# Window attention feeding a mixture of attention experts: odd value slots copied on the engines instead of by transfers, first queries and keys in longer rows, and a new work list

## The chip, the core and the metric

The kernel runs on one core of a Trainium2 chip. The core has five engines, each with an instruction stream of its own that it works through in order: TensorE (PE in the profile, its weight loads PEld), VectorE (DVE), ScalarE (ACT), GpSimd (POOL) and SyncE (SP), which here issues transfers. Matrix results land in PSUM, everything else lies in SBUF. The metric is the device time of one execution in microseconds; three executions of the kernel before gave 263.87, 266.73 and 267.94 us.

## The reference, cut to what matters

Eight batches of 576 tokens, eight heads of 64 numbers. The first half is attention in a window of 32 tokens to either side; its output, heads side by side, is the `x` (576 x 512) of the second half, a layer of four causal attention experts of which each token uses two.

```python
mask = np.abs(pos[:, None] - pos[None, :]) <= 32
attn = softmax(where(mask, scale * q @ k.T, -1e9))
x = heads_side_by_side(attn @ v)                 # (8, 576, 512)
logits = x @ w_gate                              # two best of 4 experts, softmax over the two
for e in range(4):
    q, k, v = x @ wq[e], x @ wk[e], x @ wv[e]
    ye = softmax(causal(scale * q @ k.T)) @ v @ wo[e]
    out += gate[e] * ye
```

All inputs and the output are float32 in the chip's main memory (HBM).

## The kernel before, in words

**One list sets all order.** `ORDER` is a string of some 900 steps. A step such as `sc010@26` names a function, its batch and indices, and after `@` the PSUM banks that it uses and, for a copy, the engine (`v` VectorE, `a` ScalarE, `g` GpSimd). The loop at L602 calls the functions in that order, so every engine's stream is the list filtered to that engine. Waits between engines follow from the data. PSUM is four tiles of two banks, numbered 0, 2, 4 and 6.

**One batch goes through these steps.** `lq`, `lk` load four heads (a group) of q or k into `qn`, `kn`, one row of 18 tokens (4608 bytes) per partition. `tq`, `tk` turn them with VectorE transposes into `Tqn`, `Tkn`, of which there is one buffer for each group. `sc` makes half of a group's scores (32-row matmuls, four in parallel), into two PSUM tiles; `ex` takes the exponential on ScalarE into `A`, once for each tile; `mk` multiplies with the window's mask, mostly on GpSimd. `lv` loads v. `av` multiplies `A` with `V` for 128 tokens, `un` divides by the row sum on VectorE (into `XN`), `xt` transposes on TensorE, `xf` evicts to `XTF`, `xb` rounds to bf16 `XTB`. Then the experts: `ga`, `gt`, `ge`, `gm`, `gu` are the gate; `pp` and `pe` project to queries and keys and evict them; `pv` and `ve` make the values; `ps`, `xe`, `se` are scores, exponential and the causal cut (GpSimd); `po`, `oe`, `pt`, `ot` are the weighted values, their normalising (VectorE), a transpose and its eviction; `py`, `ye`, `st` are the output projection, its eviction and the store. Batches overlap: while the experts of one batch run, the window attention of the next ones is under way.

**The value slots.** `V` has eight slots of 128 partitions. Even slot 2m holds tokens 128m to 128m+127 (`lv` m from 0 to 3); the lower half of slot 7 holds the last 64 tokens (`lv` 4). `av` needs windows that start in the middle of such a block, so odd slot 2m+1 holds in its upper 64 partitions those of slot 2m, and in its lower 64 those of slot 2m+2. `vc(b, x)` at L275 fills the odd slots of one half with two transfers from SBUF to SBUF. Each copies both the 64 numbers of a head and the two columns of ones behind them.

**Transfers are paced.** `load` at L174 issues on SyncE's queue and adds a dependence on the last TensorE instruction that stands before it in the list. A load so starts no sooner than TensorE has come to its place, and every load behind it on SyncE's queue waits too. The stores `st` are on the same queue.

**The start.** Group 0 of batch 0 is loaded with eight transfers each for q (ScalarE's queue) and k (SyncE's), in pieces of three tokens (768 bytes) per partition: `lqa`, `lqb`, `lka`, `lkb`, turned by `tqa` and so on (L297). Group 1 follows with the ordinary `lk01`, `tk01`, `lq01`, `tq01`. `s_mask` builds the mask on GpSimd; `s_pads` and `s_ones` are memsets on VectorE; `s_warm` loads ScalarE's table for the exponential.

Of the kernel before, what the change touches and what calls it, by code (L numbers as in the profile page):

```python
# [24 lines left out]
    s_mask lqa s_pads tqa lka tka lkb tkb s_ones lqb tqb lk01 tk01 lq01 sc000@02 tq01 lq10 lk10 sc001@46  # L25
    s_warm ex0010@4 ex0000@0 ex0011@6 ex0001@2 lq11 lv03 lv02 sc010@26 sc011@04 lk11 lv01 ex0101@6 ex0111@4
    ex0110@0 ex0100@2 vc01 tq10 tk10 mk0000@g mk0111@g mk0010@g mk0101@g lv04 mk0110@v tq11 lv00 wl1 vc00
    wl0 mk0011@g sc100@04 sc101@26 ex1011@6 ex1010@2 s_ident tk11 mk0100@v ex1000@0 ex1001@4 mk1001 mk1011
    av02@2 un02@2 lv10 av03@4 un03@4 mk0001@v av04@0 xt01@4 av00@2 xf01@4a un04@0 cw1@v un00@2 lv13 lv12
    lq20 av01@0 mk1000 mk1010 xt02@4 un01@0 xt00@0 xf02@4v xb01@v xb02@v cw0@v xf00@0a sc111@42 lv11 xb00@v  # L30
    sc110@60 vc11 lv14 tq20 ex1111@2 ex1110@4 ex1100@6 ex1101@0 lk20 pp010@2 pp011@6 pp000@0 pp001@4
    pe000@0v pe010@2a pe011@6a vc10 ga0@2 gt0@2 gm0@2 mk1111 mk1110 mk1101 mk1100 pe001@4a lk21 ps002@4
    ps011@0 ps013@6 xe013@6 xe011@0 ge0@2 av14@3 xe002@4 av13@6 av12@0 un14@3 gu0@2 un13@6 xt12@2 wl2
    ps010@4 xf12@2a un12@0 xe010@4 ps000@6 ps001@2 xt11@0 tk20 xe001@2 xe000@6 lq21 av11@4 sc201@26 xf11@0a
    ex2011@6 un11@4 tk21 wl3 ps003@4 xe003@4 se003 mk2011 se001 lk30 lv22 ex2010@2 cw2@a av10@0 sc200@46
    ps012@2 ex2001@6 ex2000@4 un10@0 xt10@0 xe012@2 xf10@0a lv23 lv20 lv21 tq21 xb12@v pv00@6 ve00@6a se000
    sc210@24 xb10@v xb11@g ex2101@4 mk2001 mk2000 mk2101 pv01@0 pv11@1 tk30 ve11@1v ex2100@2 pp100@6
    pe100@6a lq30 ga1@2 sc211@64 se011 lq31 cw3@a ve01@0a gt1@2 mk2010 gm1@2 ge1@2 gu1@2 pv10@0 vc20 po000@2
    ex2111@4 ex2110@6 ve10@0a vc21 pp111@6 tq30 pp101@0 oe000@2 pe101@0v se010 se013 mk2111 lv24 pe111@6a
    sc301@64 pp110@2 mk2110 lk31 lv30 ex3011@4 ex3010@6 ps101@4 ps102@0 tq31 pe110@2a mk2100 av20@6 un20@6  # L40
    av21@2 un21@2 xe102@0 xe101@4 av22@0 ps110@6 xe110@6 un22@0 lv32 lv34 sc300@24 lk40 tk31 av23@0 un23@0
    ex3001@4 ex3000@2 ps103@4 ps100@6 av24@2 xe103@4 xe100@6 pt000@3 ot000@3v lv33 un24@2 po010@4 ps112@6
    ps113@0 lq41 lq40 xt20@2 xe113@0 xe112@6 xf20@2a mk3001 xt21@0 oe010@4 pt010@4 ot010@4v xt22@5 xf22@5v
    xb22@v xf21@0a sc310@26 ex3100@2 ex3101@6 lk41 lv41 vc31 xb21@v sc311@40 ex3110@4 tk40 tq40 se101 py00@2
    se103 se100 py01@6 ye00@2a se113 ex3111@0 ye01@6a mk3011 mk3000 xb20@g pp210@4 pp201@2 pe210@4a pe201@2a
    pp200@0 tq41 pp211@4 pe211@4v po100@2 st01 lv31 pe200@0a ps202@0 xe202@0 sc400@46 oe100@2 ex4000@4 lk50
    lv42 ga2@2 ps211@4 ps111@0 ex4001@6 tk41 ps203@6 mk3101 xe203@6 mk3010 se111 mk3100 mk3111 mk3110 av34@3
    xe211@4 xe111@0 se110 se203 mk4001 vc30 gt2@2 un34@3 gm2@2 av33@6 av32@4 py02@3 un33@6 un32@4 lq51 st00
    xt32@0 pt100@1 po110@6 pv20@4 ge2@2 xf32@0a ye02@3v oe110@6 gu2@2 ot100@1a lq60 pt110@3 ot110@3v ve20@4a
    xt31@6 ps200@2 xf31@6v sc401@40 xe200@2 lq50 pv21@6 ex4011@0 xb31@v tk50 av30@2 lk60 ps201@0 ex4010@4  # L50
    ve21@6a xe201@0 un30@2 ps212@4 av31@6 py11@0 xe212@4 un31@6 lk51 st02 lv44 sc411@42 ye11@0a lv43 se201
    tq50 py10@6 ex4110@4 ex4111@2 ye10@6v xt30@0 xf30@0a sc410@24 ex4101@4 ex4100@2 sc500@60 lv51 vc41
    ps210@4 ex5000@6 ex5001@0 xe210@4 xb30@v tq51 se200 xb32@g pp301@2 pe301@2a pp300@6 pp311@0 mk4000
    mk4111 lv40 pe311@0a pe300@6a pp310@2 pe310@2a tk51 sc501@04 lv53 ga3@2 ps213@6 gt3@2 ex5010@0 ex5011@4
    ps301@0 xe213@6 ps302@4 se211 py12@3 xe301@0 ge3@2 xe302@4 st11 vc40 lv54 lk61 gm3@2 mk4010 mk4011
    mk4110 mk5001 av43@6 un43@6 gu3@2 se210 av42@0 ye12@3a un42@0 se213 mk4101 po200@4 po210@6 oe200@4
    pv30@2 oe210@6 st10 pt200@0 ot200@0v xt41@4 ve30@2a ps303@0 ps310@6 xf41@4a mk4100 mk5010 mk5000 xe310@6
    av40@2 av41@4 lv52 lq70 lv50 av44@6 lv64 lq61 xe303@0 vc50 un40@2 ps313@2 ps312@0 xe313@2 xe312@0 vc51
    un41@4 un44@6 pt210@7 st12 xt40@4 xb41@g ot210@7v xt42@6 xf40@4a xb40@g mk5011 xf42@6v xb42@v sc511@02
    ex5111@2 ex5110@0 sc510@46 mk5110 ex5101@6 ex5100@4 mk5100 se311 pp401@2 ps311@6 pe401@2a xe311@6  # L60
    ps300@0 xe300@0 ga4@4 se300 mk5101 py21@2 tq60 ye21@2a pv40@6 ve40@6a pp400@2 pp411@0 tk61 gt4@4 ge4@4
    gm4@4 tk60 gu4@4 tq61 lv61 pe400@2a ps403@2 xe403@2 ps401@6 mk5111 ps400@4 av54@2 pe411@0a se303 se310
    se301 xe400@4 xe401@6 av51@0 un54@2 pv31@3 av52@4 un51@0 un52@4 av53@6 ve31@3a av50@0 pv41@2 ve41@2a
    un53@6 se403 se313 st21 py22@3 ye22@3a sc600@64 un50@0 lv62 lv60 ex6000@6 ex6001@4 sc610@20 ex6100@2
    ex6101@0 ps402@6 xt50@4 lv63 lq71 lv74 st22 xe402@6 xf50@4a mk6001 po300@2 se400 xb50@g po310@0 xt51@6
    pp410@4 oe300@2 xf51@6a xt52@2 oe310@0 pt310@3 xf52@2v pe410@4a sc601@60 xb52@v ot310@3a ex6011@0
    sc611@24 ex6110@2 ex6010@6 ex6111@4 mk6100 xb51@g lk70 vc60 vc61 pp501@0 py20@2 ye20@2a pe501@0a mk6011
    pp500@6 pe500@6a mk6110 mk6111 ga5@4 ps413@0 xe413@0 ps412@2 tq70 tq71 xe412@2 ps410@6 lv70 st20 pt300@5
    gt5@4 ot300@5v gm5@4 lv73 pp511@0 se401 mk6010 se413 se411 mk6101 ge5@4 xe410@6 pe511@0a po400@2 oe400@2
    py31@6 mk6000 gu5@4 pp510@0 ye31@6a tk70 ps501@2 pe510@0a xe501@2 ps502@6 ps411@4 av63@0 un63@0 xe502@6  # L70
    xe411@4 av62@2 av61@6 py32@0 ye32@0a st32 un62@2 av60@4 un61@6 pv51@0 ps503@6 ps500@2 un60@4 lk71 lv72
    vc71 st31 xe503@6 av64@1 xe500@2 ve51@0v sc701@46 ex7011@6 ex7010@4 un64@1 xt62@0 xf62@0v xt60@2 xf60@2a
    xt61@6 ps511@4 ps510@0 se500 se410 po410@2 oe410@2 xb62@g xb60@g xf61@6a xb61@v tk71 xe511@4 xe510@0
    mk7010 se501 se503 pv50@6 ve50@6a pt410@0 sc700@24 ex7000@2 ex7001@4 pt400@1 po500@6 mk7011 mk7001
    mk7000 oe500@6 ot400@1v py30@2 ye30@2a ot410@0a lv71 st30 vc70 pp610@4 pp611@6 pe610@4v pe611@6a
    sc711@02 ex7111@2 ex7110@0 sc710@64 mk7111 mk7110 ex7101@4 ps610@2 pp600@0 pp601@4 ex7100@6 mk7100
    mk7101 xe610@2 pe600@0a pe601@4v ps512@2 ps611@6 xe512@2 xe611@6 av73@0 pv61@4 av72@2 un73@0 py42@5
    ps612@0 ps602@6 ve61@4a un72@2 xe612@0 av74@4 un74@4 ye42@5v xe602@6 av70@2 av71@0 un70@2 un71@0 ps513@6
    ps600@4 xe513@6 ga6@2 xe600@4 se511 se601 ps613@0 ps601@6 xe613@0 ps603@4 xe603@4 xt72@3 xe601@6 py41@0
    ye41@0a st41 xf72@3v py40@4 gt6@2 ye40@4v xt71@6 xt70@0 pt500@3 gm6@2 ge6@2 xf71@6a xf70@0v se513 se613  # L80
    se510 xb70@v xb72@g se603 se610 gu6@2 xb71@g se600 se611 pv60@4 po510@0 oe510@0 pp700@6 pe700@6v ve60@4a
    pp701@4 pp711@0 ot500@3a pt510@2 ot510@2v pp710@6 pe710@6v pe701@4a pe711@0a ps702@2 st42 st40 ps703@0
    py51@4 ye51@4v xe702@2 xe703@0 py50@6 po600@0 ps713@4 oe600@0 ye50@6a ps700@2 xe713@4 xe700@2 py52@6
    po610@4 ye52@6v pt600@7 ps701@2 oe610@4 ot600@7v xe701@2 ps712@0 xe712@0 se713 se700 se711 ga7@6 ps711@2
    ps710@4 xe710@4 pt610@7 gt7@6 pv70@0 ot610@7a ge7@6 gm7@6 gu7@6 xe711@2 ve70@0v st50 st51 py61@4 ye61@4a
    st52 se701 se710 se703 pv71@2 py60@6 ye60@6a ve71@2v po711@0 po712@2 po702@4 oe711@0 oe712@2 oe702@4
    py62@0 pt712@1 po701@2 st61 oe701@2 pt702@4 ye62@0a st60 ot702@4v pt701@0 pt711@5 ot711@5v ot701@0v
    ot712@1a py71@2 ye71@2a st62 py70@0 st71 ye70@0a st70 py72@2 ye72@2v st72
"""


@with_exitstack
def kernel(
    ctx: ExitStack,
    tc: tile.TileContext,
    q: bass.AP,
# [9 lines left out]
    nc = tc.nc  # L106
# [196 lines left out]
    def lka():  # L303
        first_load("kn", k, nc.sync, 0, 4)
# [334 lines left out]
```

## Time and profile before

| | |
|---|---|
| median of three executions | 266.73 us |
| the profiled execution, its own time | 266.66 us |
| its span from first to last instruction | 264.9 us |
| TensorE, VectorE, ScalarE, GpSimd busy | 221.9, 182.2, 148.0, 124.4 us |
| first matmul | 9.30 us |
| mean granted TensorE clock | 0.945 |
| transfers from SBUF to SBUF (`V<-V`) | 32 issues: 24 of 264 KB, 8 of 132 KB |

The page gives busy time for each engine, the span in 40 slices (6.6 us each), the groups of instructions, and the chain of work that ended last. The trace answers for any stretch in microseconds from the span's start. The profiled execution lies at the median; 1.8 us of its time lie outside the span.

### The profile page before, as it was taken

To read this page: it belongs to the slowest core of one execution; us is meant where nothing else is said; L and a number is where in the kernel's file an instruction comes from. 1 tells how busy PE (TensorE), PEld (TensorE's weight loads), DVE (VectorE), ACT (ScalarE), POOL (GpSimd) and SP (SyncE) were. 2 spreads that over 40 slices of the span, in tenths; PEclk is the share of its full clock that TensorE was granted. 3 is DMA by queue.
4 is the path that set the end of the run, shared out by engine and by line. 5 is a ranking of instruction groups with operands and counts; after the bars stand their busy time and mean duration, and the time that the engine had idled before them with its cause. 6 is when DMAs were issued, how large, how long until landed. Compare 5 with 4: busy or idle time off the path is not lost.

```text
span 264.9 us, 12355 instructions
## 1 busy us (share of the span) xinstructions
PE 221.9 (84%) x5536; PEld 177.6 (67%) x5536; DVE 182.2 (69%) x385; ACT 148.0 (56%) x223; POOL 124.4 (47%) x137
## 2 busy tenths in 40 slices
PE   0556599799898899997999895999799999998872
PEld 0545478578777668875779864887587877776540
DVE  6988756599888489888627758638673916666650
ACT  0151315569655576475583675277677786556712
POOL 5029543408760677408835394057805864331200
PEclk9985958999999999999799998899999999999987
DMA  6797897998997588988469786075915570314234
GB/s 151 224 299 195 203 206 192 229 249 241 214 244 192 147 289 202 246 305 239 113 178 252 200 206 182 2 186 166 272 30 152 153 191 5 126 55 181 72 111 178
DMA packets 60405, 48.22 MB, mean 182 GB/s; under 512 B 46016, under 2 KB 48576, under 8 KB 60352
## 3 DMA queue, kind: packets, MB, share of 16 engines
q1 hardware_dynamic: 59456, 46.84, 65.0%
q8 instruction: 43, 0.70, 1.1%
q10 hardware_dynamic: 896, 0.59, 0.9%
q14 instruction: 10, 0.08, 0.1%
HBM read 30.42 MB, written 9.44 MB: 150 GB/s over the span
## 4 chain that ended last, share of the span: by engine, by line
PE 65%; DVE 12%; DMA 9%; issue 5%; ACT 3%; SPq 3%; POOL 1%; ACTq 0%; DVEq 0%
PE PS L169 57%; PE PS L172 8%; DMA V<-in_v_dram 5%; SPq L176 2%; DMA kn<-in_k_dram 2%; DMA V<-V 2%; DVE Tkn L286 1%; ACT ATE L529 1%; DVE XTB L157 1%; DVE OE L557 1%; DVE Tqn L286 1%; DVE VE L157 1%; DVE XN L389 1%; ACT OTT L153 1%; DVE OTT L157 1%
## 5 line engine op out<-in xcount | busy, mean ns | idle before, releaser
L363 POOL TENSOR_TENSOR A<-A,MASKP 128x576 f32<-128x576 f32 x61 | 86.6, 1442 | 55.7 <-ACT A L359 55.7
L169 PE MATMUL PS<-Tqn,Tkn 32*64 32x128 f32 (+2 forms) x2560 | 48.2, 284 | 17.5 <-DVE PS L203 9.3
L529 ACT ACTIVATE ATE<-PS 128x1024 bf16<-128x1024 f32 (+1 forms) x64 | 51.1, 842 | 18.5 <-PE PS L169 15.7
L169 PEld LDWEIGHTS PS<-Tqn,Tkn 32*64 32x64 f32 x2560 | 42.6, 146 | 23.3 <-DVE PS L203 9.3
L359 ACT ACTIVATE A<-PS 128x576 f32<-128x576 f32 x64 | 37.7, 652 | 30.2 <-PE PS L169 29.4
L536 POOL TENSOR_SCALAR_AFFINE_SELECT ATE<-ATE 128x512 bf16<-128x512 bf16 (+1 forms) x48 | 24.6, 533 | 54.2 <-ACT ATE L529 54.2
L169 PE MATMUL PS<-V,A 128*64 128x65 f32 (+1 forms) x1280 | 43.1, 231 | 6.7 <-issue 4.1
L169 PEld LDWEIGHTS PS<-V,A 128*64 128x64 f32 (+1 forms) x1280 | 39.4, 139 | 10.8 <-issue 7.1
L286 DVE STREAM_TRANSPOSE Tqn<-qn 128x576 f32<-128x576 f32 x30 | 34.6, 1241 | 4.8 <-DMA qn<-in_q_dram 2.8
L286 DVE STREAM_TRANSPOSE Tkn<-kn 128x576 f32<-128x576 f32 x30 | 34.9, 1241 | 2.0 <-DMA kn<-in_k_dram 2.0
L153 ACT COPY XTF<-PS 128x1024 f32<-128x1024 f32 (+1 forms) x18 | 15.0, 855 | 18.1 <-PE PS L172 17.9
L169 PE MATMUL PS<-WO,OTT 128*128 128x512 bf16 (+1 forms) x96 | 20.8, 365 | 4.2 <-ACT ATE L529 1.5
L389 DVE TENSOR_TENSOR XN<-PS,RC 128x512 f32<-128x512 f32 x32 | 22.1, 691 | 1.1
L172 PE MATMUL PS<-ident,XN 128*128 128x128 f32 x144 | 20.6, 284 | 1.8 <-DVE OTT L157 0.6
L153 ACT COPY Y<-PS 128x1024 f32<-128x1024 f32 (+1 forms) x17 | 14.7, 863 | 11.3 <-PE PS L169 5.7
L153 ACT CAST QKE<-PS 128x576 bf16<-128x576 f32 x25 | 15.8, 651 | 7.3 <-PE PS L169 7.3
L169 PE MATMUL PS<-WV,XTB 128*128 128x256 bf16 (+1 forms) x192 | 18.8, 259 | 0.6 <-issue 0.4
L169 PE MATMUL PS<-QKE 64*128 64x64 bf16 (+4 forms) x192 | 17.0, 280 | 2.7 <-DVE G L477 2.7
L172 PEld LDWEIGHTS PS<-ident,XN 128*128 128x128 f32 x144 | 16.1, 144 | 4.6 <-DVE XN L389 1.4
L169 PE MATMUL PS<-XTB,WQ 128*128 128x288 bf16 x128 | 18.5, 286 | 0.8 <-DVE XTB L157 0.7
L169 PE MATMUL PS<-XTB,WK 128*128 128x288 bf16 x128 | 18.2, 288 | 0.0
L169 PE MATMUL PS<-VE,ATE 128*128 128x65 bf16 x480 | 17.3, 193 | 1.1 <-issue 0.5
(68 smaller groups left out, 232.1 us busy)
## 6 DMA issues: line engine op xcount, KB each, us to landing
kn<-in_k_dram SPq DMA_DIRECT2D x15, 576.0 KB, 5.1
qn<-in_q_dram SPq DMA_DIRECT2D x15, 576.0 KB, 5.2
V<-in_v_dram SPq DMA_DIRECT2D x32, 256.0 KB, 4.5
out_dram<-Y SPq DMA_DIRECT2D x16, 512.0 KB, 3.7
V<-V SPq DMA_DIRECT2D x24, 264.0 KB, 4.2
V<-V SPq DMA_DIRECT2D x8, 132.0 KB, 4.5
V<-in_v_dram SPq DMA_DIRECT2D x8, 128.0 KB, 5.2
out_dram<-Y SPq DMA_DIRECT2D x16, 64.0 KB, 2.9
```

The costliest lines, as they stand in the source:

```text
L153: nc.scalar.copy(o, i)
L157: nc.vector.tensor_copy(o, i)
L169: PACE[0] = nc.tensor.matmul(*args, **kw)
L172: PACE[0] = nc.tensor.transpose(*args)
L176: ins = nc.sync.dma_start(o, i)
L286: nc.vector.transpose(T[:, dh, :].rearrange("q (p o) -> q o p", o=18), n_[:, :, 32 * dh:32 * dh + 32])
L359: nc.scalar.activation(a_part(b, g, half, p), two(b0)[:, :, 0:HS], EXP, scale=scale_att)
L363: (nc.gpsimd if eng == "g" else nc.vector).tensor_tensor(out=ap, in0=ap, in1=MASK[:, None, HS * half:HS * half + HS].to_broadcast([128, 2, ...
L389: nc.vector.tensor_tensor(out=XN[T // 2][:, T % 2, :].rearrange("p (g h d) -> p g h d", g=2, h=4), in0=u[:, :, :, 0:64], in1=rc[:, :, :, N ...
L529: nc.scalar.activation(A[:, at:at + 2 * step].rearrange("p (e x) -> p e x", e=2)[:, :, 0:w], two(b0)[:, :, 0:w], EXP, scale=scale_moe)
L536: nc.gpsimd.affine_select(ap, ap, pattern=[[0, n], [1, w]], compare_op=IS_GE, fill=0.0, base=64 * j if c == 3 else 0, channel_multiplier=-1)
L557: nc.vector.tensor_tensor(out=OE[j][:, t0:t1, :, :].rearrange("p t e d -> p e t d"), in0=p_[:, :, :, 0:64], in1=rg[:, :, :, None].to_broad ...
```

## The change

Three edits of functions, and a new list.

```diff
-    def vc(b, x):
-        pairs = VSB[b % 2][:, :, :, :].rearrange("p (m o) h d -> p m o (h d)", o=2)
-        load(pairs[64:128, 2 * x:2 * x + 2, 1, :], pairs[64:128, 2 * x:2 * x + 2, 0, :])
-        n = 2 - x
-        load(pairs[0:64, 2 * x:2 * x + n, 1, :], pairs[0:64, 2 * x + 1:2 * x + 1 + n, 0, :])
+    def vc(b, x, eng):
+        pairs = VSB[b % 2][:, :, :, :].rearrange("p (m o) h d -> p m o h d", o=2)
+        n = 2 - x
+        copy(eng, pairs[64:128, 2 * x:2 * x + 2, 1, :, 0:64], pairs[64:128, 2 * x:2 * x + 2, 0, :, 0:64])
+        copy(eng, pairs[0:64, 2 * x:2 * x + n, 1, :, 0:64], pairs[0:64, 2 * x + 1:2 * x + 1 + n, 0, :, 0:64])
...
+    FIRST = {"qn": ((0, 9), (9, 18)), "kn": ((0, 10), (10, 18))}
+    def first_load(nm, src, q_, g, x):
+        o0, o1 = FIRST[nm][x]
+        t = NAT[nm][g][:, :, :].rearrange("p o d -> p (o d)")
+        q_.dma_start(t[:, 64 * o0:64 * o1], src[0, 4 * g:4 * g + 4, 32 * o0:32 * o1].rearrange(
+            "h (p o) d -> h p (o d)", p=32))
+    def first_turn(nm, g, x):
+        o0, o1 = FIRST[nm][x]
+        for dh in range(2):
+            nc.vector.transpose(QKT[nm][g][:, dh, 32 * o0:32 * o1].rearrange("q (p o) -> q o p", p=32),
+                                NAT[nm][g][:, o0:o1, 32 * dh:32 * dh + 32])
+    def fk(g, x):
+        first_load("kn", k, nc.sync, g, x)
+    def fq(g, x):
+        first_load("qn", q, nc.scalar, g, x)
+    def gk(g, x):
+        first_turn("kn", g, x)
+    def gq(g, x):
+        first_turn("qn", g, x)
...
             for i in range(2):
-                nc.sync.dma_start(out[b, 512:576, 256 * i:256 * i + 256], ysb(b, w)[64 * i:64 * i + 64, 0, 0:256])
+                (nc.scalar if b == B - 1 and i else nc.sync).dma_start(
+                    out[b, 512:576, 256 * i:256 * i + 256], ysb(b, w)[64 * i:64 * i + 64, 0, 0:256])
```

`vc` is now two engine copies of 64 partitions (1024 numbers each, or 512 for the second one of x = 1), of the 64 numbers alone; the ones stay from a memset. Of its 16 steps the list gives 11 to GpSimd and 5 to ScalarE. Both groups of batch 0 are loaded with `fq` on ScalarE's queue and `fk` on SyncE's, one transfer for a half: 288 tokens of q (9 in a row), 320 and 256 of k (10 and 8 in a row). The second half of the very last store goes through ScalarE's queue.

The list has the same TensorE steps in another order, with other banks. Its first steps were

```
s_mask lqa s_pads tqa lka tka lkb tkb s_ones lqb tqb lk01 tk01 lq01 sc000@02 tq01 lq10 lk10 sc001@46
s_warm ex0010@4 ex0000@0 ex0011@6 ex0001@2 lq11 lv03 lv02 sc010@26 sc011@04 ...
```

and are

```
s_mask fq00 gq00 fk10 fq10 s_ones gk10 fk11 fk00 gq10 s_warm fq11 fq01 lq10 fk01 gk00 sc010@02 lv02
sc000@46 ex0101@2 ex0000@4 ex0100@0 lv01 lk10 gk11 gq01 lv00 gk01 gq11 sc001@04 tq10 tk10 s_pads lv03
ex0010@0 ex0011@4 ex0001@6 lq11 sc011@20 lk11 wl0 sc101@64 lv04 ex0111@0 ex0110@2 mk0100@g s_ident
mk0110@v mk0111@v mk0001@g mk0000@g vc00@g mk0010@g tq11 mk0101@g vc01@a sc100@20 ex1011@4 ex1000@2 wl1
tk11 av00@4 un00@4 lk20 av01@2 ... av04@0 un01@2 un04@0 av03@6 ... av02@4 ... un03@6 un02@4 xt00@0 xt02@2 ...
xt01@4 ... sc110@26
```

Its last steps were

```
... ve71@2v po711@0 po712@2 po702@4 oe711@0 oe712@2 oe702@4 py62@0 pt712@1 po701@2 st61 oe701@2 pt702@4
ye62@0a st60 ot702@4v pt701@0 pt711@5 ot711@5v ot701@0v ot712@1a py71@2 ye71@2a st62 py70@0 st71 ye70@0a
st70 py72@2 ye72@2v st72
```

and are

```
... pv71@2 po701@0 ps713@6 ve71@2v st52 st60 oe701@0 po711@2 xe713@6 oe711@2 po702@4 se713 st61 po712@0
pt711@2 pt701@3 ot711@2a py62@6 oe702@4 pt702@7 ot701@3v py70@2 ot702@7a ye62@6a st62 ye70@2a st70 oe712@0
pt712@7 ot712@7v py71@6 ye71@6a st71 py72@0 ye72@0a st72
```

Evictions change engine here and there: GpSimd gets 16 of the 24 `xb` steps (11 before) and 62 of the 64 `mk` (61 before), ScalarE all eight of the small output evictions `ye` 2 (four before), VectorE three each of the large `ve` and `ye` 1 (one each before) and two each of the two large `xf` (one each before).

## The prediction

> **What bounds the kernel now.** I first read the page's busy times and slices, of which three rows carry it:
>
> ```profile
> PE 221.9 (84%) x5536; PEld 177.6 (67%) x5536; DVE 182.2 (69%) x385; ACT 148.0 (56%) x223; POOL 124.4 (47%) x137
> ...
> PEclk9985958999999999999799998899999999999987
> DMA  6797897998997588988469786075915570314234
> ```
>
> TensorE leads with 84%, and its clock falls to half in slices 4 and 6, early. So the mean hides stages. The view of stretches, cut at the first matmul, at the point where the first batch's window attention is through (41.8 us), and at 245 us, separates them (its columns: length, busy time and count of each engine, clock, DMA share, GB/s):
>
> ```profile
> 9.30:41.80 32.50, 23.20 (x662) 19.91 (x662) 25.44 (x40) 7.95 (x13) 14.39 (x12) 0.74 0.88 227
> 41.80:245.00 203.20, 186.30 (x4752) 150.79 (x4753) 141.81 (x292) 130.90 (x198) 104.49 (x111) 0.98 0.67 182
> 245.00:264.90 19.90, 12.41 (x129) 6.94 (x127) 8.18 (x30) 7.61 (x10) 1.79 (x4) 0.87 0.33 120
> ```
>
> TensorE is idle 9.3 us before its first matmul, 9.3 us in the start-up, 16.9 us in the long middle (8% of it) and 7.5 us at the end. The middle is close to TensorE's limit; the ends are not. What holds the start-up is in the chain of waits (start, length, what):
>
> ```profile
> 14.93 9.10 DMA V<-in_v_dram
> 24.10 0.73 SPq L176
> 24.88 1.18 SPq L176
> 26.10 0.67 SPq L176
> 26.81 3.93 DMA V<-in_v_dram
> 30.81 0.64 SPq L176
> 31.49 4.01 DMA V<-V
> ```
>
> For 20 us it runs through loads of v, then the SBUF transfers, which wait on SyncE's queue for those loads. The end, in the timeline (start, length, engine, line, operation):
>
> ```profile
> 254.27 0.42 DVE L557 TENSOR_TENSOR OE<-PS,RG 128x256 bf16<-128x256 f32 x1
> ...
> 256.43 3.55 PE L169 MATMUL PS<-WO,OTT 128*128 128x512 bf16 x11 [0.93 <-ACT OTT L153]
> ...
> 260.08 0.42 DVE L157 COPY Y<-PS 128x256 f32<-128x256 f32 x1 [4.27 <-PE PS L169]
> 261.18 1.16 SPq L597 DMA_DIRECT2D out_dram<-Y  x2
> ```
>
> All output projections of the last batch stand behind the last normalising, at half clock, then two stores are issued one after the other.
>
> **What the Trainium skill says.** "TensorE: Matmul & The Clock Gate", Part 1, says that the clock drops to half after an idle window of about 3.4 us and returns after as long a busy one; the trace agrees in kind (0.50 from 18 to 26 us, where TensorE waits often). "SBUF — State Buffer", Who interferes with whom, says that GpSimd shares a port pair with VectorE and that one blocks the other for a whole instruction in VectorE's two-port copies and two-input operations. The trace fits: a mask step on GpSimd takes 1417 ns in the median and up to 1931, a wide rounding there 1092 in the mean and up to 1472. "DMA: Bandwidth & Descriptors", Issuing engines are not separate DMA queues, says that queues of several engines share the same 16 DMA engines, so a second queue saves issue time only.
>
> **The change, part by part.**
>
> *Copies in place of transfers.* 32 issues go from SyncE (median 634 ns each), with them 7.4 MB of traffic and SyncE's waits for v loads (17.2 us, 6 times). TensorE itself waited for V<-V only 0.6 us by name, so outside the start-up I cost this gain at nothing: it was covered by scores made far ahead. The price: no row shows a float32 copy on GpSimd; the nearest is its wide rounding, 1092 ns mean for 1024 numbers. Eleven steps, 7 of x = 0 (two copies, 2.18 us) and 4 of x = 1 (1.64), are 21.8 us; with one more mask and more roundings (4 wide, 2 narrow ones of 0.29: 6.4 in all) GpSimd comes to 152.6 us, 58%. Bounds for a copy: the memset of 640 numbers took 0.63, so 1.0 for 1024 from below; the mask's rate, 1442 ns for 576, gives 2.5 from above. I take 1.09. ScalarE gets 4 x 1.55 + 2.05 = 8.2 us at its 1.02 for 1024, and loses about 4.5 of evictions: 152 us. VectorE's sum stays near 182. None becomes the bound by its sum. Behind a copy on GpSimd wait masks and causal cuts, and for these `av` and `po`.
>
> *Start.* Rows of 2304 bytes lie between 768 (about 215 GB/s, 3 to 5 us) and 4608 (311 in 18 to 20 us); I take 260. `fq10` is second on its queue and shares with as much of SyncE's, so 1.15 MB land by 2.1 + 4.4 = 6.5. VectorE: `gq00` 4.4 to 5.4 (2 x 0.50), `s_ones` 1.0, `gk10` 2 x 0.55, `gq10` 1.0: first matmul at 8.5 (before 9.30). Two `sc` at 2.16 (4.32 for the first pair before) end at 12.8. Two exponentials at 0.65 free the banks for `sc001` at 14.1; it ends at 15.7. `tq10` rewrites what that read: 15.7 to 18.0 (2.33). `lk10` is issued at about 13, after 2.95 MB of earlier loads and two v loads; at 260 GB/s and 200 for v it lands at about 18, so `tk10` ends at 20.4. `sc101`, `sc100` follow at half clock (5.43 for such a pair before), to 25.8 (before 27.3).
>
> Now VectorE holds it. `s_pads`, done in idle time before, stands here: 4.6 us, then two masks at 0.95, `tq11`, `tk11` at 2.3: its first `un` starts at 31.5. GpSimd: masks at 14.1, 17.7 and 19.1, `vc00` to 22.7, two more masks to 25.6, so `av00` starts at 25.8. `vc01` on ScalarE (1.55 after v's load) lies in the wait for `sc100`. Four `av` at 1.1 end at 30.2; `av02` waits for the bank of `un00`, to 33.5. The five `un` end near 35.8 and `xt01` at 37. Before, the same six `sc`, five `av` and three `xt` were through at 41.8: **4.8 us** earlier. Bounds: if `lk10` comes at the 227 GB/s of the whole stage, it and all behind it are 2 us later; a blocked port adds up to 0.5 to each copy and mask. Range 1 to 7.
>
> *The middle.* Same TensorE work, new order. I counted along both lists, with the mean durations of the rows, the TensorE work that stands between a step and the one that needs its result: from `av` to `xt` the median goes from 4.3 to 5.4 us, from `xt` to the first `pp` from 3.5 to 5.5, from `pp` to `ps` down from 9.1 to 7.2, from scores to `av` it stays at 13. The chain from `xt` to `pp` is an eviction (1.02) and a rounding (0.9 to 1.1), so more room helps where other work queues between. Of the 16.9 us idle, 6.8 on TensorE's matmuls is "issue", with no shown cause, and about 10 waits on other engines. I take 1 us gain, bounds 4 less and 4 more.
>
> *The end.* `po701`, `po711` are normalised first and `py70` runs beside `oe712`; behind the last normalising (254.7 by the old clock) stand only `pt712` 0.4, `ot712` 0.35, `py71` 1.7 and `py72` 0.6 at half clock, with `ye72` after `ye71` on ScalarE: about 259.0 to the last eviction, where it was 260.5. One store each on SyncE and ScalarE (nothing is queued behind) cuts 1.16 of issue to 0.6; before, 2.6 us lay between issue's end and the span's. In all **2.2 us**, bounds 0 and 3.
>
> Sum: 4.8 + 1 + 2.2 = 8.0 off 266.66, which is the median too (266.73): **258.7 us**. The terms' bounds added up (start 1 to 7, middle -4 to 4, end 0 to 3) reach from 252.7 to 269.7; taken as independent of each other, about 253 to 264.
>
> **The rivals.**
>
> *The covers hold, little is gained (no change), 0.23.* For it: the chain names V<-V for only 1.5% of the span, and the DMA share of the start-up is 0.88, so loads of q and k may set the pace. Then the start-up gives 2.5, the end 1.5, the middle 0: 262.7. That the transfers were hidden anyway belongs here: the copies then do nothing.
>
> *GpSimd comes late (slower), 0.17.* It takes its stream in order, so a copy that waits for v holds the masks behind it. Its load in a batch is 8 masks at 1.44, cuts of 3.1, copies of up to 3.8 and roundings of about 2: 20 of the 29 us that a batch takes. At 2.5 us a copy it is 25, and each lost wait reaches `av`. The gains at both ends are 7.0; to end 5.3 above the start the middle must lose 12.3, or 1.5 us in each batch: that is the point from which it decides. With 2.5 us a batch it is 266.7 - 7 + 20 = 279.7; with just 1.6, 272.5. Against it: GpSimd waits 110 us for ScalarE now, and scores stand 13 us ahead of `av`.
>
> *More is gained, inside the faster chance.* If "issue" waits come from instruction fetches that share the DMA engines, less traffic shortens them: 3 us more, 255.7.
>
> **How the numbers follow.** About 2% (5.3 us) is what a measurement of this kernel tells from no change; the three runs alone spread over 4. Forecast with its larger variant 0.60, no change 0.23, slower 0.17. The range holds 8 in 10: from 252.5 to 267.5, which leaves out most of the slower case and the largest gains.
>
> **What would show it.** Right: first matmul near 8.5; `sc110` near 37 with `V<-V` gone from the chain; copies on GpSimd near 1.1; the middle's idle share at or below 8%; the last store's issue under 0.7 us. Wrong: waits of `av` for masks or V by GpSimd over 1 us in each batch, copies above 2 us, or first loads of later batches later than now.

## The result and the profile after

The changed kernel takes 278.65 us in the median of four executions (276.45 to 281.99), the kernel before, run beside it, 265.5. The ratio is 1.048, with a 95% interval from 1.037 to 1.060: slower, where 258.7 us and faster had been forecast. Here and below, medians are of all executions, while ratios use only executions within 1.5% of the fastest one of their kernel. The profiled execution took 280.03 us, its span is 278.1, which is 13.2 more than before.

The page after, busy times and the rows of the DMA engines and of GpSimd in 40 slices (7.0 us each now):

```profile
PE 221.1 (79%) x5536; PEld 178.7 (64%) x5536; DVE 192.6 (69%) x381; ACT 151.8 (55%) x234; POOL 150.8 (54%) x166
...
POOL 5000396069249735989883669768561695160030
DMA  1532768547595857464755676235521420040345
```

Busy times are what the sums said: GpSimd 150.8 (152.6 expected), ScalarE 151.8 (152), TensorE unchanged. VectorE has 10 us more, where the sum stood still: 3.2 of them are its masks (6.2 us for two, 3.0 for three before), 2.4 are two roundings of weights (`WQ`, 1633 ns each in the place of 416), and six more wide evictions, 1.2 us each, bring most of the rest. The difference in time lies in the first slices: in the first four the DMA engines are at 1 to 5 tenths, where they were at 6 to 9 before. The chain of waits (start, length, what) goes through there:

```profile
2.35 21.99 DMA kn<-in_k_dram
24.36 0.76 DVE Tkn L303
25.16 2.52 PE PS L170 x76
27.70 0.37 SPq L177
28.12 5.07 DMA kn<-in_k_dram
...
41.73 1.29 DVE A L354
43.01 4.05 issue
47.06 0.75 DVE A L354
```

A first load of k, issued at 1.6 us, lands at 24.4. The last three lines are VectorE's two masks; the 4.05 us between them are part of the first one, and the section on VectorE's stack comes back to them. In the timeline (start, length, engine, line, operation, in brackets the wait ahead) VectorE waits for each of the first loads:

```profile
8.11 1.20 DVE L303 STREAM_TRANSPOSE Tqn<-qn 128x288 f32<-128x288 f32 x2 [7.17 <-DMA qn<-in_q_dram]
...
12.64 1.30 DVE L303 STREAM_TRANSPOSE Tkn<-kn 128x320 f32<-128x320 f32 x2 [2.34 <-DMA kn<-in_k_dram]
14.82 1.21 DVE L303 STREAM_TRANSPOSE Tqn<-qn 128x288 f32<-128x288 f32 x2 [0.87 <-DMA qn<-in_q_dram]
...
15.57 2.39 PE L170 MATMUL PS<-Tqn,Tkn 32*64 32x96 f32 x80 [15.57 <-DVE Tqn L303]
...
24.36 2.25 DVE L303 STREAM_TRANSPOSE Tkn<-kn 128x320 f32<-128x320 f32 x4 [8.34 <-DMA kn<-in_k_dram]
...
58.65 2.50 PE L170 MATMUL PS<-Tqn,Tkn 32*64 32x96 f32 x160
```

The first matmul starts at 15.6 us (9.3 before). The last line is `sc110`: by it the first batch's six `sc`, five `av` and three `xt` are through. Before, this point lay at 41.8. The view of stretches from this point to the end, before and then after (length, busy time and count of each engine, clock, DMA share, GB/s):

```profile
41.78:264.90 223.12, 198.73 (x4879) 157.75 (x4878) 150.01 (x322) 138.51 (x208) 106.28 (x114) 0.97 0.64 176
```

```profile
58.65:278.10 219.45, 195.36 (x4879) 156.09 (x4878) 158.24 (x320) 140.90 (x216) 132.75 (x142) 0.99 0.50 146
```

Both hold the same 4879 matmuls. So the start costs 16.9 us and everything behind it gains 3.7; the difference of the two is the 13.2 of the span. I had expected 4.8 us gain in the start and 3.2 behind it. TensorE's busy time behind the start falls by 3.4 us, at a granted clock of 0.99 in the place of 0.97, and its idle time stays where it was (24.1 us, 24.4 before). Most of what follows is about the start.

### The profile page after: what moved, and what is told of

Its sections match the earlier page's. It is cut to its first block, busy times and chain, and to the rows that moved or that the text cites. A ratio compares the mean times of both kernels' runs of the same rounds, so it can differ in the third digit from the quotient of the medians.

```text
span 278.1 us, 12345 instructions
## 1 busy us (share of the span) xinstructions
PE 221.1 (79%) x5536; PEld 178.7 (64%) x5536; DVE 192.6 (69%) x381; ACT 151.8 (55%) x234; POOL 150.8 (54%) x166
## 4 chain that ended last, share of the span: by engine, by line
PE 50%; DVE 25%; DMA 10%; issue 7%; ACT 4%; POOL 1%; SPq 1%; ACTq 0%; DVEq 0%; POOLq 0%
PE PS L170 43%; DMA kn<-in_k_dram 10%; PE PS L173 7%; DVE Tqn L287 5%; DVE Tkn L287 4%; DVE XTB L158 2%; DVE XN L380 2%; DVE OE L548 1%; DVE PS L446 1%; DVE ATE L212 1%; DMA out_dram<-Y 1%; DVE A L354 1%; ACT A L350 1%; ACT QKE L154 1%; DVE WQ L158 1%
## 5 line engine op out<-in xcount | busy, mean ns | idle before, releaser
L354 POOL TENSOR_TENSOR A<-A,MASKP 128x576 f32<-128x576 f32 x62 | 87.5, 1432 | 49.1 <-ACT A L350 49.1
L170 PE MATMUL PS<-Tqn,Tkn 32*64 32x128 f32 (+2 forms) x2560 | 50.3, 285 | 30.2 <-DVE Tqn L303 15.6
L170 PEld LDWEIGHTS PS<-V,A 128*64 128x64 f32 (+1 forms) x1280 | 38.8, 139 | 12.6 <-DMA V<-in_v_dram 3.8
L287 DVE STREAM_TRANSPOSE Tqn<-qn 128x576 f32<-128x576 f32 x28 | 32.4, 1240 | 0.7 <-PE PS L170 0.7
L287 DVE STREAM_TRANSPOSE Tkn<-kn 128x576 f32<-128x576 f32 x28 | 32.5, 1238 | 0.0
L156 POOL CAST XTB<-XTF 128x1024 bf16<-128x1024 f32 (+1 forms) x20 | 14.8, 758 | 31.3 <-DVE XTF L158 21.6
L154 ACT COPY XTF<-PS 128x1024 f32<-128x1024 f32 (+1 forms) x18 | 13.4, 769 | 25.9 <-PE PS L173 25.7
L156 POOL COPY V<-V 64x1024 f32<-64x1024 f32 (+1 forms) x22 | 21.2, 963 | 1.3
L170 PE MATMUL PS<-WO,OTT 128*128 128x512 bf16 (+1 forms) x96 | 19.5, 346 | 2.2 <-ACT ATE L520 1.5
L154 ACT CAST QKE<-PS 128x576 bf16<-128x576 f32 x24 | 15.1, 644 | 8.5 <-PE PS L170 8.5
L173 PEld LDWEIGHTS PS<-ident,XN 128*128 128x128 f32 x144 | 17.1, 150 | 3.8 <-issue 1.4
L170 PEld LDWEIGHTS <-ATE 128*128 128x128 bf16 x480 | 16.5, 97 | 2.6 <-issue 1.1
```

What stands on the lines that cost most here:

```text
L154: nc.scalar.copy(o, i)
L156: nc.gpsimd.tensor_copy(o, i)
L170: PACE[0] = nc.tensor.matmul(*args, **kw)
L173: PACE[0] = nc.tensor.transpose(*args)
L287: nc.vector.transpose(T[:, dh, :].rearrange("q (p o) -> q o p", o=18), n_[:, :, 32 * dh:32 * dh + 32])
L354: (nc.gpsimd if eng == "g" else nc.vector).tensor_tensor(out=ap, in0=ap, in1=MASK[:, None, HS * half:HS * half + HS].to_broadcast([128, 2, ...
```

## The experiments

Ten kernels were run after it, in three groups. Medians of the kernel before moved between 264 and 267 us from one group to the next, so I give each kernel's ratio to the runs of before beside it, with its 95% interval. "Through" is the start of `sc110` (or, in the old list, `sc111`), as above.

| kernel | ratio to before | first matmul | through |
|---|---|---|---|
| changed kernel | 1.048 [1.037, 1.060] | 15.6 us | 58.7 us |
| one transfer per head | 1.006 [1.000, 1.011] | 9.7 | 45.6 |
| old list, one transfer for four heads | 1.024 [1.015, 1.033] | 18.4 | 48.9 |
| old list, one transfer per head | too few for one; median 268.1 beside 267.4 | 9.6 | 42.2 |
| old list, V copied by engines | 1.125 [1.115, 1.135] | 9.4 | 43.7 |
| per head, `s_pads` first | 0.983 [0.978, 0.988] | 9.9 | 41.6 |
| per head, two masks to GpSimd | 1.004 [0.999, 1.009] | 9.8 | 43.3 |
| per head, both | 1.001 [0.996, 1.007] | 9.8 | 44.7 |
| per head, V by transfers | 1.127 [1.104, 1.149] | 9.7 | 46.6 |
| `s_pads` first, group 0 first | 0.981 [0.976, 0.987] | 9.9 | 38.8 |
| the same, `lq10` later | 0.990 [0.986, 0.995] | 9.9 | 40.8 |

**Theory A** was that the new first loads use few DMA engines: their source runs over four heads outermost, and heads and rows can't be joined into one dimension since only a part of the rows is read. **Theory B** was VectorE's stack of work in the new list, **theory C** the copies of V.

### The first loads, one transfer per head

```diff
-        q_.dma_start(t[:, 64 * o0:64 * o1], src[0, 4 * g:4 * g + 4, 32 * o0:32 * o1].rearrange(
-            "h (p o) d -> h p (o d)", p=32))
+        for hh in range(4):
+            q_.dma_start(t[32 * hh:32 * hh + 32, 64 * o0:64 * o1],
+                         src[0, 4 * g + hh, 32 * o0:32 * o1].rearrange("(p o) d -> p (o d)", p=32))
```

> The changed kernel with each of the eight first loads cut into four transfers, one for a head (32 partitions), same bytes, rows and queues. Theory A (a transfer whose outermost dimension is the four heads runs on 4 of the 16 DMA engines, and that alone made the change slower): DMA share from 2 to 8 us at 0.8 or more (0.25 now), first matmul at 8.5 to 9.5 us (15.6 now), time 257 to 264 us. Theory B (the new list stacks VectorE's work in the start, and its masks collide with GpSimd's): the loads come early but the time stays above 268. Theory C (the copies of V on the engines cost it): also above 268, and the middle, not the start, is slower than before.

The same stretch of the kernel before, of the changed kernel and of this one, columns as above:

```profile
2.00:8.00 6.00, 0.00 (x0) 0.00 (x0) 4.76 (x14) 1.49 (x2) 2.43 (x6) 1.00 0.84 202
```

```profile
2.00:8.00 6.00, 0.00 (x0) 0.00 (x0) 0.00 (x0) 1.49 (x2) 2.44 (x6) 1.00 0.24 81
```

```profile
2.00:8.00 6.00, 0.00 (x0) 0.00 (x0) 2.10 (x9) 1.49 (x2) 2.44 (x6) 1.00 0.78 207
```

With four heads in one transfer the DMA share is 0.24, about 4 of 16 engines, and they move 81 GB/s; with the heads apart 0.78 and 207. Too few transfers in flight are not the reason: in the changed kernel seven are issued by 4.7 us, and the share still lies between 0.22 and 0.26 in each stretch of 2 us up to 8. The first matmul comes at 9.7, `sc110` at 45.6 instead of 58.7. This is 13.1 us; the ratio falls from 1.048 to 1.006, which is some 11 us. The mechanism of theory A holds. Its "alone" doesn't: 257 to 264 us were expected and the kernel only draws level with the one before. Theory B or C had to explain some 8 us.

### The same loads in the old list

```diff
     def lka():
-        first_load("kn", k, nc.sync, 0, 4)
+        first_load("kn", k, nc.sync, 0, 0)
     def lkb():
-        first_load("kn", k, nc.sync, 4, 6)
+        first_load("kn", k, nc.sync, 0, 1)
```

`first_load` and `first_turn` are those of the change; `lqa`, `lqb` and the turns follow in the same way.

> The kernel before with its own list, but group 0 of batch 0 loaded as in the change: rows of 9 or 10 tokens, one transfer over four heads. Theory A: DMA share near 0.25 until these four loads (1.2 MB) are in, first matmul at 12 to 15 us instead of 9.3, time 268 to 272. Theories B and C: no difference beyond 1 us, about 265.5.

The second kernel has the `first_load` of the experiment above in it:

> As the run before it, but each of the four loads cut into four transfers of one head. Theory A: first matmul at 8.5 to 9.5 us and 263 to 266 us, so the longer rows themselves are harmless. If instead the longer rows or their transposes cost, it stays near the run with one transfer.

One transfer for four heads put off the first matmul to 18.4 us and cost 2.4%, some 6 us; more than expected, for in this list the memsets of PSUM (L203) stand behind the turning of all of k. The DMA share came otherwise than expected: 0.71 from 2 to 8 us, where the ordinary loads of group 1 (issued from 2.3 us on) run beside these four, and 0.27 from 14 to 18. With the heads apart the first matmul is at 9.6 and no difference from the kernel before can be seen. So the longer rows show no harm, and no help either; the DMA share and rate from 2 to 8 us are alike, too: 0.84 and 202 GB/s in the kernel before, 0.84 and 206 here.

### The copies of V, without the list and the list without the copies

In the old list, with the changed `vc` and the engine of each step as in the change:

```diff
-    ... ex0110@0 ex0100@2 vc01 tq10 ... lv00 wl1 vc00 ...
+    ... ex0110@0 ex0100@2 vc01@a tq10 ... lv00 wl1 vc00@g ...
```

> The kernel before with its own list and first loads, but V's odd slots copied by GpSimd or ScalarE, on the engines that the change names for each step. Theory A says nothing against it: 262 to 268 us. Theory C: over 271, with av waiting for masks or V. Copies of 1024 numbers on GpSimd at 1.04 us (as in the changed kernel).

It is 12.5% slower, by 33 us: for this list theory C is right, and far beyond its 271. Copies take 1.04 us as expected; the cause is in its view of waits (engine, line, what it waited for: us in total, times, longest):

```profile
POOL V L155 <- DMA V<-in_v_dram: 41.9, 6, 12.0
...
PE PS L169 <- POOL XTB L155: 12.6, 2, 8.6
...
PEld PS L169 <- POOL A L363: 7.7, 7, 2.0
```

The old list puts `vc` close behind `lv`. A transfer there waits on SyncE's queue. A copy waits in GpSimd's stream, 42 us in all, and masks and roundings behind it come late. The opposite, the new list with transfers:

```diff
-    ... mk0000@g vc00@g mk0010@g tq11 mk0101@g vc01@a sc100@20 ...
+    ... mk0000@g vc00 mk0010@g tq11 mk0101@g vc01 sc100@20 ...
```

> The run with one transfer per head, its list unchanged, but V's odd slots filled by transfers again at the places that the list has. If the copies are neutral with this list (the room that it leaves is what helps): within 2 us of that run. If the copies themselves bring the 3.5 us that are gained after the start: slower by 3 to 6 us, with loads of q, k or v late behind the transfers on SyncE's queue.

12.7% slower: the sign that was expected if the copies bring the gain, but some 32 us beside the run with one transfer per head, where 3 to 6 were expected. Its view of waits:

```profile
PE PS L170 <- DMA V<-V: 25.1, 5, 8.0
```

The new list puts `vc` far behind `lv` and close ahead of `av`, where a copy of 1 us fits and a transfer, 4.5 us from issue to landing in the median and up to 7.9, doesn't. SyncE's queue comes on top: for the first `av` TensorE waits from 30.1 us on, and the first of these transfers is issued at 32.5. Neither half of the change can be judged by itself: each list is made for its own way of filling the slots. In the changed kernel itself GpSimd idles 1.1 us in all ahead of its 18 large copies, with no load of v named as what it waited for, and what lies behind the start is no slower than before: theory C falls for the pair of copies and list.

### VectorE's stack

```diff
-    s_mask fq00 gq00 ... tq10 tk10 s_pads lv03 ...
+    s_mask s_pads fq00 gq00 ... tq10 tk10 lv03 ...
```

> The run with one transfer per head, with s_pads (4.4 us of memsets on VectorE) put back to the head of the list, where VectorE is idle until the first load lands. Theory B (what is left of the missed start is VectorE's stack): the first un starts 4 us earlier than 39.9, the first batch's xt end near 41.5, time 3 to 5 us below that run. Rival (loads of q and k or GpSimd's masks are just as late): below 1.5 us.

`sc110` moves from 45.6 to 41.6, as theory B had it, and the ratio from 1.006 to 0.983. Part of this has a cause that I had not foreseen. The timeline of the run with one transfer per head:

```profile
27.49 6.86 POOL L355 TENSOR_TENSOR A<-A,MASKP 128x576 f32<-128x576 f32 x5
...
29.46 6.17 DVE L355 TENSOR_TENSOR A<-A,MASKP 128x576 f32<-128x576 f32 x2
```

and with `s_pads` first:

```profile
25.70 2.47 DVE L355 TENSOR_TENSOR A<-A,MASKP 128x576 f32<-128x576 f32 x2
...
26.11 2.97 POOL L156 COPY V<-V 64x1024 f32<-64x1024 f32 x2
```

VectorE's two masks take 6.17 us beside a run of five masks on GpSimd, and 2.47 beside two copies of V, where they stand 3.8 us earlier. In the changed kernel they take 6.15: the first 5.48, the second 0.75, and GpSimd's run, from 39.67 to 46.52 without a gap, ends 0.6 us before the first of them does. So the memsets cost twice here: by themselves, and by pushing the masks beside that run. That GpSimd's run holds VectorE back is read from the timelines; no run changed that alone. Then I gave both masks to GpSimd, alone and with `s_pads` first:

```diff
-    mk0110@v mk0111@v
+    mk0110@g mk0111@g
```

> The run with one transfer per head, with the two masks that the list gives to VectorE (3.1 us each there, beside five masks on GpSimd) moved to GpSimd at the same place. If VectorE lost that time to the shared port: VectorE is free 6 us earlier, GpSimd's masks end 2.8 us later, the first un comes 3 to 6 us earlier, time 1 to 4 us below. If the two were slow for another reason, or GpSimd is the late one: no gain, or slower by up to 3.

> Both of the last two edits on the run with one transfer per head. If VectorE's stack explains the start: the sum of both less what GpSimd's masks then hold, first batch's xt through at 37 to 40 us, time 258 to 262 beside 267 before. Rival as above: no better than the single edits.

Alone, the profile shows `sc110` 2.3 us earlier, but the ratios (1.004 and 1.006) don't tell the two kernels apart. With `s_pads` first it is 1.8% slower than with the masks left on VectorE: GpSimd's copies and masks then end at 39.9 instead of 35.9, and `av` waits for them. They end at 40.0 with the memsets left in place, too, so that moving the memsets can gain nothing there. That `sc110` comes still later with both edits (44.7 after 43.3) lies in the matmuls of `av` themselves, 136 of which took 6.82 us in the place of 5.33; the wait ahead of them is 1.2 us in both. The sum of both edits was expected and is not there; with the masks on GpSimd it is GpSimd that is late.

### Order among the first loads

In the run with `s_pads` first, `sc001` started at 18.2 us, after waiting for the last of group 0's loads, and ScalarE's exponentials waited until 15.8 for the issues on their own queue.

```diff
-    s_ones gk10 fk11 fk00 gq10 s_warm fq11 fq01 lq10 fk01 gk00 ... gk11 gq01 lv00 gk01 gq11 sc001@04
+    s_ones gk10 fk00 fk01 gq10 s_warm fq01 fq11 fk11 lq10 gk00 ... gq01 gk01 lv00 gk11 gq11 sc001@04
```

> The run with one transfer per head and s_pads first, with the second halves of group 0 loaded and turned ahead of those of group 1 (sc001, the third step of scores, needs group 0's; in the run with s_pads first it started at 18.2 us after waiting for that load). If order among the loads is what delays it: sc001 at 15.5 to 17 us, the first batch's xt 1 to 2 us earlier than 41.6, time 0 to 2 us lower. If it is the number of issues and bytes ahead of everything: no change within 1 us.

```profile
12.40 0.65 ACT L351 ACTIVATE A<-PS 128x576 f32<-128x576 f32 x1 [4.64 <-DMA qn<-in_q_dram]
...
15.53 1.15 PE L170 MATMUL PS<-Tqn,Tkn 32*64 32x64 f32 x63 [1.28 <-ACT A L351]
...
38.84 2.50 PE L170 MATMUL PS<-Tqn,Tkn 32*64 32x96 f32 x160
```

The exponentials start at 12.4, `sc001` at 15.5, `sc110` at 38.8. The median is 258.7 us beside 264.1 for the kernel before, ratio 0.981: this kernel is faster than both, by just under 2% than the one before. Its interval overlaps that of the run with `s_pads` first, so the step between them is seen in the profile and not in the ratio.

```diff
-    fk11 lq10 gk00 ... lv01 lk10
+    fk11 gk00 ... lv01 lq10 lk10
```

> As the run before it, with the first load of batch 1 (lq10, 576 KB) moved behind sc000 in the list, so that it doesn't share the DMA engines with batch 0's loads. If bytes set the start: sc001 another 1 to 2 us earlier, but tq10 may wait for lq10 (it starts at 21.3 now); time between 1 us lower and 1 us higher.

0.990, with a median 2.2 us higher where at most 1 was expected, and `sc110` at 40.8: later. `sc001` starts at 15.1, but TensorE now waits 4.8 us for `tk10` (1.6 before). To hold batch 1's first load back only moves the wait. In this run VectorE's two masks take 6.50 us again, the second one alone 5.68, beside a copy of V and three masks on GpSimd; and here `s_pads` stands first. Taking the memsets away is therefore no sure way around it.

## Why the prediction was wrong

**The step that failed is the first one of the start**: "Rows of 2304 bytes lie between 768 (about 215 GB/s, 3 to 5 us) and 4608 (311 in 18 to 20 us); I take 260." The rate was taken from the length of the rows, and that all 16 DMA engines share the work was taken for granted. It was 81 GB/s at a share of 0.24. I had read the diff's `"h (p o) d -> h p (o d)"` and not asked what it becomes as a transfer. The Trainium skill has it: "DMA: Bandwidth & Descriptors", Why a DMA increments its semaphore by 16 and not by 1, says that a transfer issued from such a queue uses the largest number of engines up to 16 that divides the slowest dimension of both sides; with 4 heads outermost on one side, 4. The trace agrees: 0.24 is about 4 of 16, and 0.78 with one transfer per head. No rival named this, and the range ended at 267.5.

The start's 21.7 us between forecast (37.0) and result (58.7) come apart by the run with one transfer per head: 13.1 are the transfers (58.7 to 45.6). The other 8.6 stand in that run's timeline beside the forecast's own steps. `tk10` ends at 25.0 in the place of 20.4, 4.6 us late, since `sc001` and with it `tq10` are late. VectorE's two masks take 6.2 us in the place of 1.9, 4.3 more. The other steps differ by 0.3 the other way. The 4.0 us that the move of `s_pads` gains (to 41.6) are not a part of the miss as such: the forecast had these memsets in VectorE's stack at 4.6 us, and the move saves both them and the collision. The order among the loads (2.8 more, to 38.8) meets a missed step, the late `sc001`.

- *"first matmul at 8.5"*: 15.6. Even with all engines it is 9.7, for the loads moved 207 GB/s in the place of 260 and `gq10` took 1.17 us where 1.0 was taken. The "about 215" for rows of 768 bytes was read high as well: from 3 to 5 us it was 206.
- *"`s_pads` ... 4.6 us, then two masks at 0.95"*: the memsets were placed rightly and took 4.5. The masks took 6.15 instead of 1.9. The forecast had named the shared port with "up to 0.5 to each copy and mask"; it was 4.7 for one mask. The bound was too narrow: it came from the kernel before, where VectorE's masks took 0.74 to 1.28 us.
- *"`sc001` at 14.1"*: 17.5 in the run with one transfer per head, with 16 issues on ScalarE's queue and `lq10` ahead of its data or beside it; with group 0 first it is 15.5. That ScalarE's exponentials stand behind its own issues (8.1 us of wait in the run with `s_pads` first) wasn't in the sum.
- *Copies*: right. The price taken was 1.09 us; this is the group of the changed kernel (count, busy time, mean ns, idle before):

```profile
L156 POOL COPY V<-V 64x1024 f32<-64x1024 f32 x18 | 18.7, 1041 | 1.1
```

- *The gain behind the start, 1 + 2.2*: 3.7 measured, about right in sum, but in part by luck. The 1 us of the middle was to come from shorter waits; idle time fell by 0.3 us behind the start as a whole, and the gain lies in TensorE's busy time at a higher granted clock. Of the 3.7 the end is the larger part; from the last normalising to the end of the span there are 7.4 us (270.7 to 278.1), 10.2 before (254.7 to 264.9):

```profile
271.63 1.36 PE L170 MATMUL PS<-WO,OTT 128*128 128x512 bf16 x8 [0.52 <-DVE OTT L158]
...
272.69 1.29 ACT L154 COPY Y<-PS 128x1024 f32<-128x1024 f32 x2 [0.73 <-PE PS L170]
274.01 0.60 ACTq L588 DMA_DIRECT2D out_dram<-Y  x1
274.20 0.47 SPq L588 DMA_DIRECT2D out_dram<-Y  x1
```

  The two last issues lie beside each other and take 0.66 us together where 1.16 were needed. The last projections take 1.36 us, where half clock and 2.3 us had been forecast (granted clock of these stretches: 0.91, before 0.74); from the last issue to the end of the span it took 3.4 us in the place of 2.6. That the sum of the end came near its 2.2 is so owed to two errors that offset each other in part.
- *The slower rival* had the right sign and the wrong place. GpSimd is late where copies stand close behind `lv`, as the old list shows at 33 us; in the changed kernel the new list keeps them apart. That its 279.7 us lies beside the measured 278.65 is chance: what it had lose the time, the middle, lost none.
- *"That the transfers were hidden anyway ... the copies then do nothing"*: not so for this list. Transfers in it cost 12.7% against the kernel before.

## What to carry to other kernels

Before pricing a transfer by bytes or row length, write down its outermost dimension on both sides after everything that can be joined is joined, and read the DMA share in the stretch where it runs; a share that stays at 4 of 16 while several loads are queued, as here (0.22 to 0.26), points to the shape of the transfers and not to the length of their rows. Where a list or schedule is made anew together with an operation, price the pair, for the old schedule with the new operation may be far worse than either. Work that was done in idle time is not free to move, and what stands behind it may then meet another engine.

## What the runs showed of the hardware

VectorE's two-input operation in SBUF stood beside gapless work of GpSimd and ended 0.6 us after it, in three runs. In the changed kernel and with one transfer per head it was a run of five two-input operations, and VectorE's took 5.48 and 5.50 us, 4.7 beyond its own 0.75; each of GpSimd's took its usual 1.40 us. With `lq10` later it was a copy and three such operations, and VectorE's took 5.68. In the kernel before, a mask on VectorE inside such a run took 1.28 us at most, and GpSimd's four then took 6.20, where four at the pace of the run of five would take 5.5. "SBUF — State Buffer", Who interferes with whom, of the Trainium skill says that a VectorE instruction with two SBUF inputs contends with a GpSimd instruction that reads SBUF, and calls their shared port pair an exclusive lock. The traces fit that, but the wait here is longer than any single instruction of GpSimd's. Why VectorE was let in at one time and not at the other was not tried.
